# Windowed attention with a softplus layer: values in two 64-column tiles, w_out in four pieces, v loaded later

## The chip, the cores and the metric

The kernel runs on one core of one Trainium2 chip. The metric is the time of one execution in microseconds (us) of device time, as the median of several runs. A profiled execution gives a trace: every instruction of the five engines (PE is TensorE's matmul, PEld its weight load, DVE is VectorE, ACT ScalarE, POOL GpSimd, SP the queue that issues most DMAs), with the DMA packets and the clock that TensorE was granted. Times inside the trace are counted from the start of its span.

## What is computed

The reference in short: windowed attention with eight global positions over 8 batches, 8 heads, 576 positions and 64 elements a head, then a layer of width 2048 with softplus, from 4608 tokens of 512 back to 512.

```python
scores = q @ k.T / sqrt(64)                      # per batch and head
mask = |i - j| <= 32  or  i is global  or  j is global
attn = softmax(where(mask, scores, -1e9))
x = (attn @ v), heads side by side               # [4608, 512]
out = softplus(x @ w_in) @ w_out                 # w_in [512, 2048], w_out [2048, 512]
```

## The kernel before

A **unit** is 64 positions of one batch with all heads: 9 units a batch, 72 in all. A **group** (n4) is four units, and a **token tile** (m) is two groups, so 512 tokens, nine tiles in all. The head pairs are p = 0 to 3.

For each batch: k and q are loaded in bf16 by POOL's DMA queue (load_qk, L226; a cast rides in the DMA), v by SP's queue in float32 (load_v, L215), five pieces. POOL casts v into vA (add_cast, L446) and two DMAs on SP copy it, shifted by 64 positions, into vB (shift, L453 and L454). PE picks the rows of the global positions from k and q (pick, L473, 32-column tiles), and turns k and q (tk, L515; tq, L523, both in 64-column tiles); ACT or DVE copy the results into kx and qz.

For each unit: PE computes scores of 128 keys and 8 global keys (sc, L631, s), DVE adds the mask and takes the maximum (top, L637), ACT takes the exponential (ex, L658), DVE sums and inverts (su, L666 to L668), POOL normalises (no, L674, pn, and gc, L678), PE transposes (tp, L684) and ACT or DVE copy to pt. For each batch the global rows have a path of their own (add_global): scores sg (L557), mx on DVE (L564), exponentials gexp on ACT (L571), transposes tg (L585), values ov (L596), oz on DVE (L602).

For each group the **value stage** (val, L716 to L736) computes attention times v, turned, into xo. It accumulates, for each head pair, a product with the global values (L727, up to 256 columns wide) and one per unit with vA or vB (L734, 64 columns wide). In the kernel before each product is four matmuls of 128 rows and 32 output columns, one for each 32-column tile of the array:

```python
for c in range(4):
    r, h = slice(c * 32, (c + 1) * 32), slice(c // 2 * G, (c // 2 + 1) * G)
    nc.tensor.matmul(out=xo[r, y, x, :], lhsT=vw[:, p * P + c * 32:p * P + (c + 1) * 32],
                     rhs=PS["pt", n4 * 4 + x][:, p, h], start=False, stop=(x == e_ - 1))
```

xo is copied to xT (xev). For each token tile the layer follows (add_moe): first (h, L769), 16 chunks of 4 matmuls with w_in; softplus on ACT (L774); second (o, L779), for each of four 128-token rows 16 accumulating matmuls with w_out; then a copy (oev) and an output DMA from SP (L786).

The order of the work is not that of the loops. Every piece is a job with costs for the engines that can do it, dependences, a rank and buffers that it opens (`_Order.add`, L37), and `_Order.run` (L77) lays the jobs out greedily by its own estimate: at each step the job that can start first, and among these the one with the lowest rank, gets its engine. Each engine then works its list in that order and waits at the head of it. The estimate of a DMA job is its `moves` behind what its queue still has to move, plus `slack`. `SWITCH` (95 ns) is what the planner counts when PE changes from narrow tiles to the whole array and back, 1290 ns for a change of ACT's function table.

At the start of the kernel the queue of POOL carries k and q of batch 0, w_in in four pieces (L809), k and q of batch 1, then w_out in four pieces as one job (weights_out, L811), which waits for v of batch 1 in the plan; SP's queue carries v of batch 0, vB of batch 0, v of batch 1. A `hold` (L819) is a tiny DMA on SP that reads a tile just loaded, so that what is queued behind it on SP starts only when that tile has landed: v of batch 1 is held by q of batch 1.

Of the kernel before, what the change touches and what calls it, by code (L numbers as in the profile page):

```python
# [18 lines left out]
class _Order:  # L19
# [17 lines left out]
    def add(self, cost, emit, deps=(), rank=5, opens=(), uses=(), table=None, moves=0, tiled=False, slack=0):  # L37
# [39 lines left out]
    def run(self, free):  # L77
# [74 lines left out]
def kernel(  # L152
# [88 lines left out]
    nc.vector.tensor_copy(ident_b[:], ident[:])  # L241

# [182 lines left out]
    def add_load(b, which, deps):  # L425
        if which == 2:
            T["load", b, 2] = [o.add({"DMA": (100, 0)}, lambda e, x=x: load_v(b, x), deps, rank=0,
                                     opens=[("in_v", ("in", b, 2, x))], moves=1200, slack=3000 if b > 1 else 0) for x in range(NT5)]
            return
# [3 lines left out]
                                     lambda e: load_qk(b, which) if b else None, deps + early, rank=0, moves=4300, slack=4000 if b > 1 else 0)]  # L433

    def add_cast(b, engines):
# [19 lines left out]
        T["shift", b] = o.add({"DMA": (100, 0)}, shift, T["cast", b, 2] + early, rank=0, moves=1500, slack=2000 if b > 1 else 0)  # L455

    def add_prep(b, gate, rank):
# [38 lines left out]
        for n, ws in enumerate(steps):  # L496
            T["pick", b, n] = o.add({"PE": (460 * len(ws) + 190, 460 * len(ws) + 300)}, lambda e, ws=ws: pick(e, ws),
                                    [T["load", b, w][0] for w in ws] + [T.get(("pick", b, n - 1))], rank=4, tiled=True,
# [11 lines left out]
        for p in range(HP):  # L510
# [29 lines left out]
            T["tk", b, p] = o.add(mm(QR, NQ), tk, [T["load", b, 1][0], *gate], rank=rank, tiled=True, opens=[("tk", ("tk", b, p))])  # L540
            T["kev", b, p] = o.add({"ACT": (635, 720), "DVE": (800, 880)}, kev, [T["tk", b, p], *late, *blanks["g"]],
                                   rank=3, uses=[("tk", b, p)])
            T["tq", b, p] = o.add(mm(QR, NQ), tq, [T["load", b, 0][0], *gate], rank=rank, tiled=True, opens=[("tq", ("tq", b, p))])
# [5 lines left out]
    def add_global(b, gate, early):  # L549
# [55 lines left out]
        T["sg", b] = o.add({"PE": (390, 600)}, sg, ready + early, rank=3, tiled=True,  # L605
                           opens=[("sg", ("sg", b, 0)), ("sg", ("sg", b, 1)), ("small", ("m2", b))])
        both = [("sg", b, 0), ("sg", b, 1)]
        T["mx", b] = o.add({"DVE": (1114, 1300)}, mx, [T["sg", b]], rank=2, uses=both + [("m2", b)])
# [5 lines left out]
        T["ov", b] = o.add({"PE": (393, 600)}, ov, [T["lge", b], *T["cast", b, 2], T.get(("ones_g", b))], rank=3, tiled=True, opens=[("ov", ("ov", b))])  # L614
# [87 lines left out]
    def add_values(n4):  # L702
# [13 lines left out]
        def val(e):  # L716
            for half in range(2):
                xo = PS["xo", n4, half] = psum(("xo", n4, half), [P, 2, 4, G], FP32)
                for y in range(2):
                    p = half * 2 + y  # L720
                    u = 0
                    while u < 4:
                        b, j = divmod(n4 * 4 + u, NJ)
                        e_ = min(4, u + NJ - j)
                        for c in range(4):
                            r, h = slice(c * 32, (c + 1) * 32), slice(c // 2 * G, (c // 2 + 1) * G)
                            nc.tensor.matmul(out=xo[r, y, u:e_, :], lhsT=oz[b % 2][:, p, r],  # L727
                                             rhs=PS["R", n4][:, u:e_, h], start=True, stop=False)
                        for x in range(u, e_):
                            jx = j + x - u  # L730
                            vw = vA[b % 2][:, jx // 2, :] if jx % 2 == 0 else vB[b % 2][:, jx // 2, :]
                            for c in range(4):
                                r, h = slice(c * 32, (c + 1) * 32), slice(c // 2 * G, (c // 2 + 1) * G)
                                nc.tensor.matmul(out=xo[r, y, x, :], lhsT=vw[:, p * P + c * 32:p * P + (c + 1) * 32],  # L734
                                                 rhs=PS["pt", n4 * 4 + x][:, p, h], start=False, stop=(x == e_ - 1))
# [18 lines left out]
        T["val", n4] = o.add({"PE": (1030, 1190)}, val_, ready, rank=0, tiled=True,  # L754
# [7 lines left out]
    def add_moe(m, exps):  # L762
# [48 lines left out]
    def weights_out(e):  # L811
        for a in range(KF // 4):
            nc.gpsimd.dma_start(out=w_out_t[a][:, :, :],
                                in_=moe_w_out[a * 4 * P:(a + 1) * 4 * P, :].rearrange("(a p) m -> p a m", p=P))
# [13 lines left out]
    T["w_in"] = o.add({"POOL": (2150, 0)}, weights_in, [T["load", 0, 2][3]], rank=0, moves=10800)  # L828
# [14 lines left out]
    add_load(1, 2, [hold("w", [*T["load", 1, 0], T["shift", 0]], qn[1][0:1, 0, 0:16])])  # L843
    T["w_out"] = o.add({"POOL": (3000, 0)}, weights_out, [T["load", 1, 2][3]], rank=1, moves=12500)
# [18 lines left out]
    def make_batch(b, gate, rank):  # L863
# [12 lines left out]
    for m in range(len(TILES)):  # L876
# [8 lines left out]
        if m == 0:  # L885
            add_ones(1, [T["su", 5]])
# [9 lines left out]
        if nb < B:  # L896
            make_batch(nb, [T["ex", us[-1]]], 5)
# [31 lines left out]
```

## Time and profile before

| | us |
|---|---|
| median of three runs (402.34 to 409.56) | 404.95 |
| the profiled execution | 402.19 |
| its span, first to last instruction | 400.4 |
| PE busy (5152 matmuls) | 366.4 |
| ACT busy | 288.0 |
| DVE busy | 256.3 |
| POOL busy | 146.8 |

The page's strip cuts the span into 40 slices of about 10 us and gives each engine's busy share in tenths. A row of the timeline has the start, the time from the first start to the last end, engine, line, operation, the tiles as output <- input, the form, how many instructions are merged into it, and in brackets how long the engine had stood before it and what released it; "issue" means that the trace shows nothing it could have waited for. A row of the windows has the stretch and its length, then busy time and instruction count of PE, PEld, DVE, ACT and POOL, the granted clock, the share of the 16 DMA engines' time, and GB/s. A row of the groups ends with busy time, mean ns of one instruction, and the idle time before them. Matmuls overlap: what one adds to the time is the distance from its start to the next one's, not its own length.

### The profile page before, as it was taken

How to read it: one execution, taken by the hardware profiler on the slowest of the kernel's cores; microseconds unless marked ns; L12 is line 12 of the kernel's file. 1: busy time of each engine (PE TensorE's matmuls, PEld its weight loads, DVE VectorE, ACT ScalarE, POOL GpSimd, SP SyncE). 2: the span in 40 equal slices, each digit the busy share in tenths (PEclk: the TensorE clock that was granted, in tenths of full speed). 3: DMA queues.
4: the chain of work that ended last, by engine and by line, in shares of the span. 5: the costliest groups of instructions: out<-in, count | busy, mean ns of one | idle time of the engine just before them, and what ended most of it. 6: DMA issues, size and time to landing. Idle time of an engine off the chain costs nothing.

```text
span 400.4 us, 12909 instructions
## 1 busy us (share of the span) xinstructions
PE 366.4 (91%) x5152; PEld 204.6 (51%) x5152; DVE 256.3 (64%) x1093; ACT 288.0 (72%) x707; POOL 146.8 (37%) x265
## 2 busy tenths in 40 slices
PE   1866996996999999989999999999999999999996
PEld 1634752553555645555456545554466455545442
DVE  5798673854669837999488647984886478333011
ACT  2787668773589968967698769966997589595510
POOL 8986351680017700764146003830480036022000
PEclk9999999998999999999999999999999999999999
DMA  6899699959110394059758101079111011001012
GB/s 94 148 209 167 126 161 198 190 126 173 28 54 31 86 185 102 28 146 169 143 116 133 45 0 52 31 130 188 55 42 41 11 71 56 2 26 54 2 52 79
DMA packets 59467, 37.54 MB, mean 94 GB/s; under 512 B 42000, under 2 KB 53264, under 8 KB 59408
## 3 DMA queue, kind: packets, MB, share of 16 engines
q1 hardware_dynamic: 44176, 23.08, 23.3%
q0 software_dynamic: 15232, 13.65, 22.3%
q8 instruction: 40, 0.66, 0.7%
q14 instruction: 19, 0.16, 0.1%
HBM read 36.71 MB, written 9.44 MB: 115 GB/s over the span
## 4 chain that ended last, share of the span: by engine, by line
PE 61%; DVE 16%; DMA 7%; ACT 6%; issue 5%; POOL 4%; SPq 0%; DVEq 0%; POOLq 0%; ACTq 0%
PE h L769 31%; PE o L779 15%; DMA kn<-in_k_dram 6%; DVE sm L666 5%; PE s L631 3%; PE tp L684 3%; PE tk L515 2%; DVE rs L668 2%; ACT L571 2%; PE xo L727 2%; PE tq L523 2%; DVE st L637 2%; ACT pe L658 2%; PE xo L734 2%; POOL vA L446 2%
## 5 line engine op out<-in xcount | busy, mean ns | idle before, releaser
L674 POOL TENSOR_TENSOR pn<-pe,rs 128x512 bf16<-128x512 f32 x72 | 74.8, 1038 | 197.6 <-DVE rs L668 184.9
L779 PE MATMUL o<-wout,g 128*128 128x512 bf16 x576 | 142.0, 382 | 0.0
L769 PE MATMUL h<-xT,win 128*128 128x512 bf16 x576 | 138.3, 381 | 3.5 <-issue 3.5
L774 ACT ACTIVATE g<-h 128x512 bf16<-128x512 f32 x144 | 84.5, 597 | 54.8 <-PE h L769 46.7
L658 ACT ACTIVATE pe<-st,nb 128x136 f32<-128x136 f32 x288 | 92.9, 401 | 6.8 <-POOL gw L678 4.6
L637 DVE CUSTOM_DVE_ANT_0 st<-s,mask 128x136 f32<-128x136 f32 x288 | 70.1, 295 | 27.7 <-PE s L631 26.0
L769 PEld LDWEIGHTS <-win 128*128 128x128 bf16 x576 | 53.5, 98 | 55.4 <-issue 4.8
L779 PEld LDWEIGHTS <-g 128*128 128x128 bf16 x576 | 53.2, 98 | 50.2 <-issue 1.6
L666 DVE TENSOR_REDUCE sm<-pe 128x4 f32<-128x544 f32 x67 | 47.8, 713 | 12.0 <-ACT pe L658 11.7
L684 PE MATMUL tp<-ident_b,pn 128*128 128x128 bf16 x288 | 30.0, 231 | 9.6 <-POOL pn L674 6.8
L631 PE MATMUL s<-kx,qz 128*128 128x136 bf16 x288 | 35.5, 235 | 0.9 <-ACT qz L419 0.3
L631 PEld LDWEIGHTS <-qz 128*128 128x128 bf16 x288 | 24.4, 103 | 20.7 <-issue 4.1
L446 POOL CAST vA<-v 128x512 bf16<-128x512 f32 (+3 forms) x48 | 28.4, 611 | 16.9 <-DMA v<-in_v_dram 15.7
L684 PEld LDWEIGHTS <-pn 128*128 128x128 bf16 x288 | 19.6, 102 | 27.5 <-POOL pn L674 23.3
L419 DVE COPY osb<-o 128x512 f32<-128x512 f32 x18 | 12.4, 687 | 30.2 <-PE o L779 30.2
L419 DVE COPY qz<-tq 64x576 bf16<-64x576 bf16 x32 | 24.1, 753 | 4.8 <-PE tq L523 4.5
L637 DVE DVE_READ_ACCUMULATOR2_ANT nb<- 128x1 f32 x288 | 23.9, 83 | 0.0
L419 ACT COPY pt<-tp 128x512 bf16<-128x512 bf16 x34 | 19.4, 580 | 4.8 <-PE tp L684 4.7
L668 DVE TENSOR_SCALAR rs<-rs,notg 128x4 f32<-128x4 f32 x72 | 21.2, 294 | 2.6
L419 ACT COPY qz<-tq 64x576 bf16<-64x576 bf16 x32 | 20.4, 636 | 2.9 <-PE tq L523 2.6
L419 DVE COPY pt<-tp 128x512 bf16<-128x512 bf16 x38 | 15.9, 420 | 6.6 <-PE tp L684 6.2
L727 PE MATMUL xo<-R,oz 128*32 128x256 bf16 (+3 forms) x384 | 19.2, 259 | 0.3 <-DVE R L419 0.3
(120 smaller groups left out, 397.8 us busy)
## 6 DMA issues: line engine op xcount, KB each, us to landing
out_dram<-osb SPq DMA_DIRECT2D x36, 256.0 KB, 2.0
v<-in_v_dram SPq DMA_DIRECT2D x24, 256.0 KB, 7.1
kn<-in_k_dram POOLq DMA_DIRECT2D x8, 576.0 KB, 9.7
qn<-in_q_dram POOLq DMA_DIRECT2D x8, 576.0 KB, 12.9
vB<-vA SPq DMA_DIRECT2D x16, 256.0 KB, 3.8
v<-in_v_dram SPq DMA_DIRECT2D x16, 192.0 KB, 4.6
win<-in_moe_w_in_dram POOLq DMA_DIRECT2D x4, 512.0 KB, 9.6
wout<-in_moe_w_out_dram POOLq DMA_DIRECT2D x4, 512.0 KB, 12.2
```

The source lines that it names most:

```text
L419: (nc.scalar.copy if e == "ACT" else nc.vector.tensor_copy)(out, in_)
L446: nc.gpsimd.tensor_copy(to[r], at[r])
L631: nc.tensor.matmul(out=ps[:, y, :], lhsT=qz[i][:, x * 2 + y, j, :, :], rhs=kf[:, x * 2 + y, j * W:j * W + EXT], start=True, stop=True)
L637: nc.vector.tensor_tensor_reduce(out=PS["st", n][:, p, :], in0=PS["s", n, x][:, y, :], in1=mask[:, j, :], scale=-SCALE, scalar=3.0e38, op0 ...
L658: nc.scalar.activation(out=pe[:, p, 0:EXT], in_=PS["st", n][:, p, :], func=AF.Exp, bias=PS["nb", n][:, p:p + 1], scale=-1.0, **({"accum_ou ...
L666: nc.vector.reduce_sum(out=sm[:], in_=PS["pe", n][:, :, 0:EXT], axis=AX)
L668: nc.vector.tensor_scalar(out=rs[:], in0=rs[:], scalar1=notg[:, j:j + 1], scalar2=None, op0=OP.mult)
L674: nc.gpsimd.tensor_tensor(out=pn[:].rearrange("c p (a s) -> c p a s", a=2), in0=wide[:, :, :, 0:G], in1=rs[:].unsqueeze(2).unsqueeze(3).to ...
L684: nc.tensor.transpose(out=ps[:, p, :], in_=PS["pn", n][:, p, :], identity=ident_b[:])
L769: nc.tensor.matmul(out=h[:, :], lhsT=w_in_t[kd][:, c * P:(c + 1) * P], rhs=PS["xT", m][:, kd, :], start=(kd == 0), stop=(kd == KD - 1))
L774: nc.scalar.activation(out=t[:, :], in_=PS["h", m, c][:, :], func=AF.Softplus)
L779: nc.tensor.matmul(out=PS["o", m, ns][:, :], lhsT=PS["g", m, kf][:, ns * P:(ns + 1) * P], rhs=w_out_t[kf // 4][:, kf % 4, :], start=(kf == ...
```

## The change

The value stage uses two tiles of 64 columns in place of four of 32, so each product is two matmuls. The planner knows the two widths as 32 and 64 and counts SWITCH between them as well. w_out is four jobs, placed by units 4 to 7 of the plan, behind the second k and q in POOL's queue, and each second-layer matmul depends on its own piece; v of batch 1 is held by the second piece of w_out. The third k and q depend on the last piece of w_out. A small activation of its own (Exp on one column of zeros) stands at the head of ACT, and the planner starts with the exp table loaded. mx of batch 0 comes behind the scores of two units; the second ones job and the preparation of batch 1 change their dependence and rank; some loads get other slacks.

```diff
-        table = None
-        tiled = False
+        table = "exp"
+        tiled = 0
...
-                    t = max(t0, free[e] + (self.SWITCH if e == "PE" and tiled and not j["tiled"] else 0))
+                    t = max(t0, free[e] + (self.SWITCH if e == "PE" and tiled and tiled != j["tiled"] else 0))
...
-                if j["tiled"] and not tiled:
+                if not tiled and j["tiled"]:
...
+    warm = temp([P, 1], FP32, "warm")
+    nc.vector.memset(warm[:], 0.0)
+    nc.scalar.activation(out=warm[:], in_=warm[:], func=AF.Exp)
...
-                                     opens=[("in_v", ("in", b, 2, x))], moves=1200, slack=3000 if b > 1 else 0) for x in range(NT5)]
+                                     opens=[("in_v", ("in", b, 2, x))], moves=1200, slack=(0, 1500, 3000)[min(b, 2)]) for x in range(NT5)]
...
-        T["mx", b] = o.add({"DVE": (1114, 1300)}, mx, [T["sg", b]], rank=2, uses=both + [("m2", b)])
+        T["mx", b] = o.add({"DVE": (1114, 1300)}, mx, [T["sg", b], T["top", 1, 1] if b == 0 else None], rank=2, uses=both + [("m2", b)])
...
-                        for c in range(4):
-                            r, h = slice(c * 32, (c + 1) * 32), slice(c // 2 * G, (c // 2 + 1) * G)
+                        for h in range(2):
+                            r = slice(h * D, (h + 1) * D)
                             nc.tensor.matmul(out=xo[r, y, u:e_, :], lhsT=oz[b % 2][:, p, r],
-                                             rhs=PS["R", n4][:, u:e_, h], start=True, stop=False)
+                                             rhs=PS["R", n4][:, u:e_, h * G:(h + 1) * G], start=True, stop=False)
...
-                            for c in range(4):
-                                r, h = slice(c * 32, (c + 1) * 32), slice(c // 2 * G, (c // 2 + 1) * G)
-                                nc.tensor.matmul(out=xo[r, y, x, :], lhsT=vw[:, p * P + c * 32:p * P + (c + 1) * 32],
-                                                 rhs=PS["pt", n4 * 4 + x][:, p, h], start=False, stop=(x == e_ - 1))
+                            for h in range(2):
+                                r = slice(h * D, (h + 1) * D)
+                                nc.tensor.matmul(out=xo[r, y, x, :], lhsT=vw[:, p * P + h * D:p * P + (h + 1) * D],
+                                                 rhs=PS["pt", n4 * 4 + x][:, p, h * G:(h + 1) * G], start=False,
+                                                 stop=(x == e_ - 1))
...
-                             [T["soft", m, kf], T["w_out"], last, T["first", m, KF - 1] if m < len(TILES) - 1 else None],
+                             [T["soft", m, kf], T["w_out", kf // 4], last, T["first", m, KF - 1] if m < len(TILES) - 1 else None],
...
-    add_load(1, 2, [hold("w", [*T["load", 1, 0], T["shift", 0]], qn[1][0:1, 0, 0:16])])
-    T["w_out"] = o.add({"POOL": (3000, 0)}, weights_out, [T["load", 1, 2][3]], rank=1, moves=12500)
...
-                add_load(b, w, [T["no", (b - 2) * NJ + 2], T["shift", b - 1]])
+                add_load(b, w, [T["no", (b - 2) * NJ + 2], T["shift", b - 1] if b > 2 else T["w_out", KF // 4 - 1]])
...
-            add_ones(1, [T["su", 5]])
+            add_ones(1, [T["su", NJ - 1]])
+            for a in range(KF // 4):
+                T["w_out", a] = o.add({"POOL": (760, 0)}, lambda e, a=a: weights_out(a),
+                                      [T["no", 4 + a], T.get(("w_out", a - 1))], rank=1, moves=3100, slack=2000)
+            add_load(1, 2, [hold("w", [T["w_out", 1], T["shift", 0]], w_out_t[1][0:1, 0, 0:16])])
...
-            make_batch(nb, [T["ex", us[-1]]], 5)
+            make_batch(nb, [T["ex", us[-1]]], 4 if nb == 1 else 5)
```

As built, the order on PE changes mostly in the first token tiles. In the first, eight h stand ahead of the second pick, and 16 o of the tile's second layer stand directly behind its h, ahead of tg of batch 1; three and eight more o follow, then pick of batch 2 and ov. POOL issues the four w_out pieces between the units' normalisations (two behind unit 5, one behind unit 6, one behind unit 8), and the third k and q directly behind the last.

More of the change, by code (lines that the diff above doesn't have):

```diff
@@ L432, in add_load @@
         T["load", b, which] = [o.add({"POOL" if b else "DMA": (880 if b else 0, 0)},
-                                     lambda e: load_qk(b, which) if b else None, deps + early, rank=0, moves=4300, slack=4000 if b > 1 else 0)]
+                                     lambda e: load_qk(b, which) if b else None, deps + early, rank=0, moves=4300, slack=(0, 2500, 4000)[min(b, 2)])]
     def add_cast(b, engines):
@@ L454, in shift @@
             nc.sync.dma_start(out=vB[b % 2][64:P, :, :], in_=vA[b % 2][0:64, 1:NT5, :])
-        T["shift", b] = o.add({"DMA": (100, 0)}, shift, T["cast", b, 2] + early, rank=0, moves=1500, slack=2000 if b > 1 else 0)
+        T["shift", b] = o.add({"DMA": (100, 0)}, shift, T["cast", b, 2] + early, rank=0, moves=1500, slack=(0, 1000, 2000)[min(b, 2)])
     def add_prep(b, gate, rank):
@@ L826 @@
     add_load(0, 2, [hold("v", T["load", 0, 1], kn[0][0:1, 0, 0:16])])
-    T["w_in"] = o.add({"POOL": (2150, 0)}, weights_in, [T["load", 0, 2][3]], rank=0, moves=10800)
+    T["w_in"] = o.add({"POOL": (2150, 0)}, weights_in, [T["load", 0, 2][3]], rank=0, moves=10800, slack=1500)
     for w in (1, 0):
```

21 lines of the change are left out of this document (10 added, 11 removed).

## The prediction

> **What bounds the kernel.** I read the page's first two parts, then the timeline of TensorE (PE), then windows around each place where PE stood, and last the DMA issues on SP and POOL.
>
> ```profile
> span 400.4 us, 12909 instructions
> PE   1866996996999999989999999999999999999996
> q8 instruction: 40, 0.66, 0.7%
> ```
>
> From 40 us on nearly every tenth of the PE strip is a 9: behind the start, PE's own work sets the time. What can be gained is therefore where PE stands, where it runs at half clock, or work taken out of its queue. The strip dips in slice 6 and slice 9. The timeline of PE shows both, and two smaller ones of the second kind:
>
> ```profile
> 58.68 4.48 PE L769 MATMUL h<-xT,win 128*128 128x512 bf16 x20
> 65.80 0.71 PE L585 MATMUL tg<-ident_b,pg 128*128 128x128 bf16 x5 [2.65 <-ACT pg L571]
> 67.10 0.46 PE L596 MATMUL ov<-vA,lg 128*32 128x128 bf16 x20 [0.58 <-DVE lg L419]
> 67.74 3.59 PE L779 MATMUL o<-wout,g 128*128 128x512 bf16 x9
> 71.55 2.57 PE L779 MATMUL o<-wout,g 128*128 128x512 bf16 x11
> 77.75 0.21 PE L727 MATMUL xo<-R,oz 128*32 128x64 bf16 x4
> ...
> 91.79 0.81 PE L769 MATMUL h<-xT,win 128*128 128x512 bf16 x3
> 96.13 2.29 PE L769 MATMUL h<-xT,win 128*128 128x512 bf16 x5 [3.53 <-issue]
> ...
> 223.74 0.45 PE L523 MATMUL tq<-ident_b,qn 72*64 72x72 bf16 x16 [0.93 <-issue]
> ...
> 297.34 0.39 PE L515 MATMUL tk<-ident_b,kn 72*64 72x72 bf16 x12 [0.61 <-issue]
> ```
>
> Gap A, at 63 us: after the last h of the first token tile, PE waits 2.65 us for ACT's global exponentials and 0.58 us for DVE, then runs nine o in 3.59 us where the next eleven take 2.57. Gap B, at 92.6: 3.53 us in which nothing that the profile shows is waited for, then five h in 2.29 us where twenty took 4.48 before. The windows say why the matmuls behind both gaps are slow:
>
> ```profile
> 40.00:44.00 4.00, 4.00 (x152) 3.50 (x154) 2.63 (x14) 2.60 (x8) 0.00 (x0) 1.00 0.14 25
> 52.00:78.00 26.00, 22.68 (x180) 11.14 (x181) 15.75 (x75) 18.64 (x45) 9.26 (x15) 0.93 1.10 186
> 68.00:70.00 2.00, 2.00 (x7) 0.78 (x6) 1.81 (x7) 1.75 (x6) 1.16 (x2) 0.55 1.22 196
> 70.00:72.00 2.00, 2.00 (x10) 0.96 (x9) 1.34 (x4) 1.30 (x4) 0.61 (x2) 0.60 1.22 196
> 96.00:98.00 2.00, 1.87 (x5) 0.71 (x5) 0.00 (x0) 0.60 (x1) 0.00 (x0) 0.50 1.32 170
> ```
>
> The third number from the end is the granted clock: 0.55 and 0.60 behind gap A, 0.50 behind gap B. Both lie where the DMA share (next to last) is over 1.1. B I read as a late instruction fetch: the instruction queue fetches in 40 packets through the same loaded engines, and the gaps of 0.93 and 0.61 us "issue" also follow a value stage with 16-matmul transposes directly behind it, the places with most instructions per us. That reading is inferred; no row names it.
>
> **The change, part by part.**
>
> *Values in two column tiles.* The stage issues half as many matmuls. What a group of four 32-column matmuls takes, and what a pair of 64-column ones takes, stand in these rows of PE (the tk and tq transposes use 64-column tiles now):
>
> ```profile
> 85.14 0.28 PE L727 MATMUL xo<-R,oz 128*32 128x256 bf16 x4
> 85.25 0.20 PE L734 MATMUL xo<-pt,vB 128*32 128x64 bf16 x4
> ...
> 85.37 0.28 PE L727 MATMUL xo<-R,oz 128*32 128x256 bf16 x4
> ...
> 89.49 0.63 PE L473 MATMUL pick<-qn,pick 72*32 72x128 bf16 x32
> 89.95 0.62 PE L473 MATMUL pick<-kn,pick 72*32 72x128 bf16 x32
> 90.50 0.71 PE L523 MATMUL tq<-ident_b,qn 72*64 72x72 bf16 x32
> 91.04 0.69 PE L515 MATMUL tk<-ident_b,kn 72*64 72x72 bf16 x32
> ```
>
> Between 85.25 and 85.37 four groups start: 30 ns a group, 7 ns a matmul, so the four tiles run together. tq to tk: 0.54 us for 16 pairs, 34 ns a pair of 72 columns; scaled to 64 columns 30. The wide group (256 columns, 85.14 to 85.25) takes 0.11 us, 0.43 ns a column, 27.5 ns for 64. So a pair is bounded by 27.5 and 34 against 30 now. How many groups there are:
>
> ```profile
> L727 PE MATMUL xo<-R,oz 128*32 128x256 bf16 (+3 forms) x384 | 19.2, 259 | 0.3 <-DVE R L419 0.3
> ...
> L734 PE MATMUL xo<-pt,vA 128*32 128x64 bf16 x640 | 18.5, 199 | 0.0
> L734 PE MATMUL xo<-pt,vB 128*32 128x64 bf16 x512 | 17.6, 199 | 0.0
> ...
> L515 PEld LDWEIGHTS <-kn 72*64 72x64 bf16 x512 | 12.2, 124 | 3.9 <-issue 1.8 <-DMA kn<-in_k_dram 1.4
> L734 PEld LDWEIGHTS <-vA 128*32 128x32 bf16 x640 | 14.5, 101 | 0.1
> ```
>
> (640+512)/4 = 288 narrow groups: 288 x (27.5 to 34, less 30) = -0.7 to +1.2 us for the whole kernel. I take 0: halving the matmuls by itself buys nothing, because they already overlap. What it does buy is a mode switch: 32-column pick to 64-column tq costs 0.55 where pick to pick costs 0.46, so 0.09 us; in the order as built ten value stages now stand directly beside a tk or tq, 10 x 0.09 = -0.9 us. And PE's instruction stream loses 768 matmuls with their weight loads, all in the densest stretches: I take the gaps of 0.93 and 0.61 away, -1.5 us (ends 0 and -1.5).
>
> [...]
>
> *w_out in four pieces behind the second q, v of that batch beside it.* These rows carry it:
>
> ```profile
> 20.60 17.64 DMA kn<-in_k_dram
> ...
> 42.00 0.54 SPq L821 DMA_DIRECT2D held<-qn  x1
> 42.58 4.46 SPq L219 DMA_DIRECT2D v<-in_v_dram  x5
> ...
> 49.23 3.09 POOL L813 DMA_DIRECT2D wout<-in_moe_w_out_dram  x4
> ...
> DMA to landing us min/median/max: 6.1/12.2/16.6
> ...
> 54.22 0.86 POOL L227 DMA_DIRECT2D qn<-in_q_dram  x1
> ...
> DMA to landing us min/median/max: 24.0/24.0/24.0
> ...
> 54.17 20.67 SPq L219 DMA_DIRECT2D v<-in_v_dram  x5
> ...
> DMA to landing us min/median/max: 7.7/8.4/9.1
> ...
> 79.35 3.08 POOL L446 CAST vA<-v 32x512 bf16<-32x512 f32 x5
> ```
>
> (First landing row: w_out's four; second: the third q; third: the two vB copies of batch 1.) Batch 1's q lands at 42.0; then the DMA engines are nearly idle (share 0.14 in 40 to 44) until v, and POOL's queue moves nothing before 49.2. w_out lands from 55.3 to 68.1, (68.1-55.3)/3 = 4.3 us a piece. Behind the q its pieces would land at about 46, 50, 55 and 59, and the third k and q, queued behind them, at about 64 and 69. So 16 o can stand ahead of tg, and in the order as built they do, then 3 and 8 more before ov, with pick between. Gap A goes: 2.65 + 0.58, and the half clock behind it, 3.59 less 9 x 2.57/11 = 2.10, so 1.5: together -4.7 us. The filler isn't lost to later stages: from 67 to 92 PE never stood, so every o done early shortens that stretch, as long as ACT, DVE and POOL bring the units.
>
> What is late next is v of batch 1. It is issued when the second w_out piece has landed, near 50 instead of 42.6, and must be cast by POOL before ov, copied into vB before the third value stage, and in POOL's queue its casts stand ahead of the first pn of the stage. Alone v is quick; beside POOL's queue it starves: the third v, issued from 54.17, was cast only at 79.35, when the q of 54.22 had landed (78.2). If bytes are conserved: 17 + 10 us of w_out, k and q with half of v beside them, the rest of v done by about 69. PE reaches ov near 70. That is tight; pick, which needs the third q at 69, as well. I take +1.5 us, ends 0 and the price of the rival below. SP: the first out goes ahead of vB's copies, ready near 67, so they wait for the cast, not for it.
>
> POOL now issues four pieces of 0.77 us between the units 5 and 9: 3.1 us later for the last pn of the second value stage. Cover: in the order that stage stands behind tk of batch 1, which waits for k to land at 38.2 either way; I take 0, without that cover 3.1. The eight h that now go ahead of the second pick are work moved, not removed: 0. With these queues drained by 69, loads and fetches of the 92 us stretch start against a shorter backlog, and the dense stretch before it has half its value matmuls and pick no longer in it: I take gap B as gone, 3.53 and 2.29 less 5 x 4.48/20 = 1.2, -4.7 us; ends 0 and -4.7.
>
> *Exp table, mx, ranks, slacks.* ACT already loads one table at its start and none before the first exponential, so the warm use removes nothing: one memset and one activation under the first k load, 0. mx behind two units' scores gives ACT an earlier start under the same k load, 0. The switch and slack numbers only move the order; from the fifth tile's second layer on it is the same as before but for the value stages.
>
> Sum: -0.9 - 1.5 - 4.7 - 4.7 + 1.5 = -10.3 us. The profiled execution took 402.19 us (span 400.4), so 391.9. The median of the runs is 404.95, 2.8 above it; shifted with it the sum is 394.6. I predict between, 393.
>
> **The rivals.**
> 1. *Gap B stays or moves.* Against it the thinner stream; for it, k, q and v of batch 3 still go out together near 85, and the order still has value, tk, tq directly there. Then 393 + 4.7 = 398. Chance 0.17.
> 2. *A new wait takes A's place*, at pick or ov, with about the same length and the same half clock: 393 + 4.7 = 398. For it, the 69 against 70. Chance 0.10.
> 3. *v starves: slower.* If v of batch 1 needs as long beside w_out, k and q as the third v (25 us from issue to cast), it is cast at 75 to 78 and vB lands 8.4 later, at 83.5 to 86.5; the third value stage, at 77.75 now, comes 6 to 9 us late, and nothing is left to fill. With B's fetch in the same congestion nothing else is won: 405 + 6 to 9 = 411 to 414. It decides from v's last cast after 69 (then vB's 8.4 us end at 77.75). Against it: v's own bytes are small and POOL's queue is done near 69. Chance 0.11.
> 4. *Pairs bound by weight loads.* The row of 64-column loads has 124 ns against 101: 23 ns more, unhidden in 384 groups (288 and 384/4) = 8.8: 402. Chance 0.05; the tq row speaks against it. [...]
> 5. *Every matmul has its price.* At tq's 17 ns a matmul, 768 fewer give 13: 380. Chance 0.03; 7 ns a matmul speaks against it. [...]
>
> **How the numbers follow.** The forecast has 0.54; its own range is 387 (no new wait, loads a little earlier) to 397 (one of the small terms 0, 1.5 more of wait). The range takes in 1, 2 and 4: 386 to 404. Outside lie 3 and 5 and a little of the forecast, under 0.2. A measurement of this kernel tells about 2% from no change, 396.9 to 413. Faster: 0.54 less 0.02, rival 5, and a few hundredths of 1 and 2: 0.58. Slower: half of rival 3 and a rest, 0.07. Within: 0.35.
>
> **What would show it.** Value stage: groups of two near 30 ns apart, its length unchanged but for the switch. A: no idle time before tg after the first tile, clock 1.0 in 60 to 72, o at 61 to 65. w_out landed by 60. v of batch 1 cast by 69 and ov without wait; a wait there on POOL vA or at pick on the q is rival 2 or 3. B: no "issue" of over 1 us on PE between 80 and 100. Wrong would be the prediction if PE stands as long as before in other places, above all between 66 and 78.

## The result and the profile after

The kernel after takes 389.71 us (median of four runs, 389.29 to 389.95), the kernel before 407.25 beside it on the same chip (four runs, 402.34 to 410.08). The ratio is 0.9654, 95% interval [0.9598, 0.9709]: 3.5% faster. Ratios here and below leave out runs that lie over 1.5% above the fastest of their kernel, so beside the widely scattered runs of the kernel before a ratio and the quotient of two medians need not agree.

What PE waited for without a visible cause stands first in the waits (engine, line and what it waited for: total us, how often, the longest). Of the kernel before:

```profile
PE h L769 <- issue: 3.5, 1, 3.5
...
PE tq L523 <- issue: 1.3, 2, 0.9
...
PE tk L515 <- issue: 0.6, 1, 0.6
```

And all that is left of it in the kernel after, and three lines of its page:

```profile
PE xo L739 <- issue: 0.3, 1, 0.3
```

```profile
span 387.8 us, 11381 instructions
...
PE   1945999999998999999999999999999999999996
...
q8 instruction: 34, 0.56, 0.6%
```

5.4 us of "issue" have become 0.3, the dip of slice 9 is gone, and the instruction queue fetches 34 packets in place of 40. The other dip, behind the first token tile, is gone as well; the timeline of PE and two windows of the kernel after:

```profile
61.54 1.89 PE L775 MATMUL h<-xT,win 128*128 128x512 bf16 x8
63.26 3.62 PE L785 MATMUL o<-wout,g 128*128 128x512 bf16 x16
66.72 0.44 PE L590 MATMUL tg<-ident_b,pg 128*128 128x128 bf16 x5
...
70.72 0.47 PE L601 MATMUL ov<-vA,lg 128*32 128x128 bf16 x20
...
72.20 0.40 PE L689 MATMUL tp<-ident_b,pn 128*128 128x128 bf16 x4 [0.25 <-POOL pn L679]
```

```profile
60.00:72.00 12.00, 11.96 (x149) 6.44 (x146) 7.03 (x35) 10.31 (x30) 4.07 (x7) 1.00 0.26 62
...
80.00:100.00 20.00, 19.50 (x279) 11.40 (x277) 15.24 (x70) 16.40 (x35) 9.54 (x16) 1.00 0.67 126
```

Sixteen o fill the place where PE stood 2.65 us for tg, and the granted clock is 1.00 in both windows.

### The profile page after: what moved, and what is told of

Same layout as the page of the kernel before. It is cut to its first block, busy times and chain, and to the rows that moved or that the text cites. A ratio compares the mean times of both kernels' runs of the same rounds, so it can differ in the third digit from the quotient of the medians.

```text
span 387.8 us, 11381 instructions
## 1 busy us (share of the span) xinstructions
PE 360.8 (93%) x4384; PEld 203.8 (53%) x4384; DVE 256.1 (66%) x1086; ACT 289.1 (75%) x716; POOL 147.2 (38%) x265
## 4 chain that ended last, share of the span: by engine, by line
PE 51%; DVE 18%; ACT 10%; DMA 7%; POOL 5%; issue 4%; SPq 4%; DVEq 0%; POOLq 0%; ACTq 0%
PE h L775 25%; PE o L785 12%; DVE sm L671 5%; ACT pe L663 5%; DMA v<-in_v_dram 5%; SPq L219 4%; DVE rs L673 3%; PE s L636 3%; DVE st L642 3%; PE tp L689 2%; DMA qn<-in_q_dram 2%; POOL pn L679 2%; POOL vA L451 2%; PE xo L732 2%; PE xo L739 2%
## 5 line engine op out<-in xcount | busy, mean ns | idle before, releaser
L785 PE MATMUL o<-wout,g 128*128 128x512 bf16 x576 | 140.1, 379 | 0.0
L671 DVE TENSOR_REDUCE sm<-pe 128x4 f32<-128x544 f32 x67 | 47.8, 713 | 12.4 <-ACT pe L663 12.1
L636 PE MATMUL s<-kx,qz 128*128 128x136 bf16 x288 | 34.0, 234 | 0.4 <-POOL vA L451 0.3
L424 DVE COPY qz<-tq 64x576 bf16<-64x576 bf16 x36 | 27.1, 753 | 3.0 <-PE tq L528 2.5
L424 ACT COPY pt<-tp 128x512 bf16<-128x512 bf16 x37 | 21.4, 586 | 4.9 <-PE tp L689 4.8
L673 DVE TENSOR_SCALAR rs<-rs,notg 128x4 f32<-128x4 f32 x72 | 21.7, 301 | 2.7 <-DVE rs L672 0.2
L732 PE MATMUL xo<-R,oz 128*64 128x256 bf16 (+3 forms) x192 | 19.8, 263 | 1.2 <-ACT R L424 0.7
L582 DVE TENSOR_TENSOR s<-s 128x1 f32<-128x1 f32 x8 | 1.3, 158 | 28.1 <-ACT pg L576 28.1
L739 PE MATMUL xo<-pt,vA 128*64 128x64 bf16 x320 | 19.1, 201 | 0.0
## 6 DMA issues: line engine op xcount, KB each, us to landing
wout<-in_moe_w_out_dram POOLq DMA_DIRECT2D x4, 512.0 KB, 11.6
```

The costliest lines, as they stand in the source:

```text
L424: (nc.scalar.copy if e == "ACT" else nc.vector.tensor_copy)(out, in_)
L636: nc.tensor.matmul(out=ps[:, y, :], lhsT=qz[i][:, x * 2 + y, j, :, :], rhs=kf[:, x * 2 + y, j * W:j * W + EXT], start=True, stop=True)
L671: nc.vector.reduce_sum(out=sm[:], in_=PS["pe", n][:, :, 0:EXT], axis=AX)
L673: nc.vector.tensor_scalar(out=rs[:], in0=rs[:], scalar1=notg[:, j:j + 1], scalar2=None, op0=OP.mult)
L785: nc.tensor.matmul(out=PS["o", m, ns][:, :], lhsT=PS["g", m, kf][:, ns * P:(ns + 1) * P], rhs=w_out_t[kf // 4][:, kf % 4, :], start=(kf == ...
```

## The experiments

All medians, with the range of the runs. The kernel before ran beside them on the same chip: it took 405.23 (402.11 to 414.26) beside the first four, 403.50 (396.21 to 409.54) beside the next four, 404.13 (398.34 to 405.45) beside the last four.

| run | us | range | ratio to before |
|---|---|---|---|
| e1_after_four_tiles | 399.64 | 395.54 to 401.15 | 0.9870 [0.9803, 0.9937] |
| e2_before_two_tiles | 394.81 | 394.64 to 396.46 | 0.9765 [0.9722, 0.9809] |
| e3_after_w_out_late | 393.72 | 393.62 to 394.10 | 0.9742 [0.9705, 0.9778] |
| e6_before_w_out_early | 400.97 | 397.75 to 404.74 | 0.9919 [0.9871, 0.9966] |
| e8_four_tiles_beside_tk | 399.27 | 397.45 to 402.57 | 0.9992 [0.9937, 1.0047] |
| e9_four_tiles_elsewhere | 389.29 | 388.31 to 390.35 | 0.9696 [0.9631, 0.9762] |
| after_again | 389.27 | 388.61 to 389.69 | 0.9694 [0.9633, 0.9755] |
| e4_kq_before_w_in | 389.13 | 388.62 to 389.68 | 0.9689 [0.9611, 0.9766] |
| e10_e8_without_late_loads | 393.68 | 392.95 to 394.26 | 0.9799 [0.9727, 0.9870] |
| e11_after_without_late_loads | 389.39 | 389.00 to 389.50 | 0.9689 [0.9604, 0.9775] |
| e7_v_held_by_q | 389.15 | 388.91 to 389.47 | 0.9688 [0.9635, 0.9741] |
| e5_no_exp_warm | 394.73 | 390.88 to 395.49 | 0.9800 [0.9724, 0.9876] |

### The two halves of the change, each alone

**The value tiles put back, the rest of the change kept** (e1_after_four_tiles; the planner still counts 64-column tiles, so the order on every engine is that of the kernel after):

```diff
-                        for h in range(2):
-                            r = slice(h * D, (h + 1) * D)
+                        for c in range(4):
+                            r, h = slice(c * 32, (c + 1) * 32), slice(c // 2 * G, (c // 2 + 1) * G)
...
```

> The changed kernel with its order unchanged, but each product of the value stage again four 32-column matmuls (the planner still told 64, so that no other instruction moves). Theory 'stream': the gaps called issue went because PE has 768 fewer matmuls to fetch; then one to four gaps of 0.3 to 3.5 us come back, 392 to 396 us in all, some with the label issue on PE between 84 and 100 us. Theory 'load': they went because w_out, k, q and v are queued otherwise; then no such gap over 0.5 us and only the switches come back, 9 x 0.09 = 0.8, less 18 x 0.045 that the pairs are slower inside (936 ns a stage against 894): 389.7 us, no change. In either case the stage by itself is shown to be worth nothing if its inner length falls back to 894 ns and its exit to 123 ns.

**The value tiles alone, on the kernel before** (e2_before_two_tiles; the same edit the other way round in the value stage of the kernel before, its order kept):

> The kernel before with its order unchanged, but each product of the value stage two 64-column matmuls. Theory 'stream': gap B (3.5 us and 1.4 of half clock) and the gaps of 0.9 and 0.6 us go, span near 394 us. Theory 'load': gap B stays, span 399.5 to 401 us, and only the two small gaps may go. Gap A (2.65 us before tg, 0.58 before ov, half clock behind) stays in both.

**w_out early alone, on the kernel before** (e6_before_w_out_early; four tiles; for the changed jobs the planner lays out another order):

```diff
...
-    add_load(1, 2, [hold("w", [*T["load", 1, 0], T["shift", 0]], qn[1][0:1, 0, 0:16])])
-    T["w_out"] = o.add({"POOL": (3000, 0)}, weights_out, [T["load", 1, 2][3]], rank=1, moves=12500)
...
+            for a in range(KF // 4):
+                T["w_out", a] = o.add({"POOL": (760, 0)}, lambda e, a=a: weights_out(a),
+                                      [T["no", 4 + a], T.get(("w_out", a - 1))], rank=1, moves=3100, slack=2000)
+            add_load(1, 2, [hold("w", [T["w_out", 1], T["shift", 0]], w_out_t[1][0:1, 0, 0:16])])
```

> The kernel before with only w_out in four pieces behind the second q and v held by its second piece; value stage, table and slacks as before. My theory: gap A goes, and since the loads around 85 to 100 us move as well, part of gap B: span 391 to 396 us. Rival 'values': most of the 12.6 us come from the value stage and its instruction stream, so 396 to 399 us with gap B still there.

The four corners: 405.23 before, 400.97 with w_out early (-4.3; 1.4 to 5.2 by the interval of the ratio), 394.81 with two tiles (-10.4), 389.7 with both and the small parts (-15.5, where the two alone add up to -14.7). The tiles are the greater part, in either order: 399.64 less 389.71 is 9.9. The median of e1 lies above the 392 to 396 that its theory 'stream' expected (its profiled execution, 395.54, within). The span of e6, 398.2, misses the 391 to 396 of its first theory and lies in the 396 to 399 of the rival 'values'.

That the two add up does not mean that each is worth this by itself. e5 (below) has both halves and the small parts and only lacks the planner's flag for the exp table with its activation; it takes 394.73, no less than e2. It has no gap A either, but its first h starts at 49.03, where that of e2 starts near 46.3. So beside two tiles w_out early paid only with the order that the flag is argued to bring.

Of these kernels those with four tiles spread over 5.6 to 12 us, those with two over less than 2. Below, e5 spreads over 4.6 with two tiles, and e10, with four tiles in half of the stages but without the later loads, over 1.3. The waits of PE say where the time was; first e1 (four tiles), then e6 (four tiles), then e2 (two tiles):

```profile
PE h L774 <- issue: 3.1, 4, 2.1
...
PE tk L520 <- issue: 1.6, 2, 1.3
...
PE o L784 <- issue: 0.5, 3, 0.2
```

```profile
PE tq L523 <- issue: 2.2, 1, 2.2
PE tk L515 <- issue: 2.0, 2, 1.4
...
PE o L779 <- issue: 1.1, 4, 0.6
...
PE h L769 <- issue: 0.8, 2, 0.5
```

```profile
PE o L780 <- issue: 1.0, 6, 0.2
```

With four tiles there are stops of up to 2.2 us, the long ones in tk, tq or the h soon behind them. In e2 none is over 0.2 us, and its six of that size are no stops: its trace holds 4334 matmuls and 4384 weight loads, so records of matmuls are missing. (The longest in another two-tile kernel is 0.6 us, in e4 below.) Gap B is gone in e2 though its w_out is as late as before. In e6, whose w_out is early, the stop at the place of gap B is down to 0.26 us, but others come: its stops of over 0.25 us make 5.6 us in all, those of the kernel before 5.4. So what gap B cost hung on the tiles; with w_out early and four tiles the stops only lie elsewhere. Gap A hung on w_out. The rows of e6, of e2 and of e5:

```profile
69.96 3.62 PE L779 MATMUL o<-wout,g 128*128 128x512 bf16 x16
73.41 0.44 PE L585 MATMUL tg<-ident_b,pg 128*128 128x128 bf16 x5
```

```profile
65.98 0.82 PE L585 MATMUL tg<-ident_b,pg 128*128 128x128 bf16 x5 [2.65 <-ACT pg L571]
```

```profile
67.66 3.62 PE L782 MATMUL o<-wout,g 128*128 128x512 bf16 x16
71.11 0.44 PE L587 MATMUL tg<-ident_b,pg 128*128 128x128 bf16 x5
```

**w_out back behind v, the rest of the change kept** (e3_after_w_out_late):

```diff
+    add_load(1, 2, [hold("w", [*T["load", 1, 0], T["shift", 0]], qn[1][0:1, 0, 0:16])])
+    for a in range(KF // 4):
+        T["w_out", a] = o.add({"POOL": (760, 0)}, lambda e, a=a: weights_out(a),
+                              [T["load", 1, 2][3] if a == 0 else T["w_out", a - 1]], rank=1, moves=3100, slack=2000)
...
-            for a in range(KF // 4):
-                T["w_out", a] = o.add({"POOL": (760, 0)}, lambda e, a=a: weights_out(a),
-                                      [T["no", 4 + a], T.get(("w_out", a - 1))], rank=1, moves=3100, slack=2000)
-            add_load(1, 2, [hold("w", [T["w_out", 1], T["shift", 0]], w_out_t[1][0:1, 0, 0:16])])
```

> The changed kernel, but w_out's four pieces are again behind v of batch 1, and v is held by q as before. My theory: w_out then lands 8 to 10 us later, 55 to 68 us, nine and not sixteen o stand ahead of tg, and 3 to 5 us of the gain go: 393 to 396 us. Rival: the gain comes from the order (table, switch, slacks) and not from where w_out is: 389 to 391 us.

It costs 4.0 us against the kernel after. The timeline of PE shows nine o where sixteen stood, and three waits:

```profile
63.18 2.11 PE L785 MATMUL o<-wout,g 128*128 128x512 bf16 x9
65.99 0.71 PE L590 MATMUL tg<-ident_b,pg 128*128 128x128 bf16 x5 [0.70 <-ACT pg L576]
...
70.12 0.40 PE L689 MATMUL tp<-ident_b,pn 128*128 128x128 bf16 x4 [0.31 <-POOL pn L679]
...
72.75 0.40 PE L689 MATMUL tp<-ident_b,pn 128*128 128x128 bf16 x4 [0.94 <-POOL pn L679]
```

These make 1.95 us against 0.25 in the kernel after; the rest of the 4.0 is spread over many waits behind 80 us, none of them over 1.2. The planner answers the later w_out with another order, so the 4.0 us are the price of both.

### Why four tiles stop PE: by position

The instruction queue's packets are 16 KB (0.66 MB in the 40 of the kernel before). The kernel before gives PE 10304 matmuls and weight loads and has 40 packets, the kernel after 8768 and 34: 1536 fewer instructions in 6 packets fewer, so 256 in a packet. If a packet is late, four tiles must hurt where PE uses up a packet fast, so where a value stage and the 64 small transposes of tk and tq follow each other, and not where the same stage stands between h and o. Two kernels put the four tiles back in nine of the eighteen value stages each, with after's order:

```diff
+            FOUR = (1, 3, 5, 8, 9, 10, 11, 12, 14)     # e8; e9 has (0, 2, 4, 6, 7, 13, 15, 16, 17)
...
-                        for h in range(2):
-                            r = slice(h * D, (h + 1) * D)
+                        w = 32 if n4 in FOUR else D
+                        for c in range(P // w):
+                            r, h = slice(c * w, (c + 1) * w), c * w // D
...
```

> The kernel after, with the four 32-column tiles back in nine of the eighteen value stages: those that have tk or tq as a direct neighbour (368 matmuls more than after; order and loads as after). Theory 'stream' (PE stands because the next packet of its instructions is late, where a value stage and the 64 small transposes of tk and tq use up a packet in under 2 us): all of the loss of about 10 us that four tiles everywhere cost in this order (399.6 against 389.7) comes back here, so 396 to 402, the runs several us apart, and waits of 'issue' of 1 us and more on PE within a few us behind these stages. Theory 'per matmul' (each 32-column matmul costs its own time wherever it stands): half of the loss, 394 to 395, with no 'issue' waits. Theory 'nothing' (the four-tile kernel lost its time for another reason): 389.7.

> The kernel after, with four 32-column tiles back in the other nine value stages, those that stand between o, tp, h and s and not beside tk or tq (400 matmuls more than after, so a few more than the run before has). Theory 'stream': these stages have long matmuls on both sides, so a packet lasts several us; about after's time, 389 to 391, runs within 1 us, 'issue' on PE under 1 us in all. Theory 'per matmul': a little over half of the loss, 394 to 396.

> The kernel after, unchanged, beside the other kernels of this call on the same chip. All theories: 389 to 391 and runs within 1 us, if the difference between chips is small.

e8, with 368 matmuls more, loses all of it: 399.27 against 389.27 of the kernel after on the same chip. e9, with 400 more, loses nothing: 389.29. The range of e8 and that of e9 are 7 us apart. A price for each matmul is excluded. (The nine stages of e8 also pay the change from 32 to 64 columns, 0.09 us each, which those of e9 don't: 0.8 of the 10.) One stop of e8, on its timeline of PE, and the clock behind it:

```profile
209.93 0.43 PE L520 MATMUL tk<-ident_b,kn 72*64 72x72 bf16 x16
210.19 0.29 PE L528 MATMUL tq<-ident_b,qn 72*64 72x72 bf16 x7
214.88 0.51 PE L528 MATMUL tq<-ident_b,qn 72*64 72x72 bf16 x9 [4.40 <-issue]
```

```profile
215.00:220.00 5.00, 4.78 (x31) 3.01 (x33) 2.67 (x7) 0.60 (x1) 0.00 (x0) 0.50 0.08 17
```

PE stops after the seventh of sixteen equal transposes, with nothing to wait for, and runs at half clock behind the stop while the DMA engines are nearly idle (share 0.08). So here the half clock follows a long stop without loaded engines. In the DMA view of e8, the stretch from 207.9 to 212.6 has no packet of the instruction queue, and the next 1.1 us have one:

```profile
DMA packets 160, 0.20 MB, mean 181 GB/s; under 512 B 7, under 2 KB 133, under 8 KB 159
...
q8 instruction: 1, 0.02, 5.4%
```

The packet starts at 212.69, when PE has stood for over 2 us, and is there at 213.64; PE goes on at 214.88, 1.24 us later. In the kernel before it is the same at gap B: packet from 93.56 to 94.67, PE again at 96.13.

All the stops show it. In the fourteen profiled executions PE has 24 waits on "issue" of over 0.25 us. Counted in blocks of 128 weight loads, which with as many matmuls are 256 instructions, each of the 24 begins at 0.67 to 0.73 of a block, so at one place of the block whatever PE is doing there, and each ends 1.2 to 1.6 us after a packet of the instruction queue has landed. No packet starts earlier than some 1.2 blocks before PE needs it.

From this the course of a packet can be estimated. When it is asked for is not in the trace; as an estimate from these starts the ask is put at 0.625 of a block, some 1.1 blocks before PE needs the packet. 57 of 489 packets start earlier than that, so the ask is rather too late, and the second and third column are rough, to about 1 us. The places that matter (us; "used up" is the life of the packet that PE then works on, "landed" is from the ask to the end of the transfer):

| kernel, place | used up in | landed after (estimate) | PE stood |
|---|---|---|---|
| before, 88.3 | 3.1 | 6.4 | 3.53 |
| e1, 210.3 | 3.7 | 4.0 | 1.25 |
| e8, 207.8 | 2.3 | 5.8 | 4.40 |
| e10 (below), 206.4 | 2.3 | 2.7 | 1.48 |
| after, 205.0 | 5.4 | 4.6 | 0.33 |

By this estimate PE stands where landing, and the 1.2 to 1.6 us after it, take longer than the packet lasts. With four tiles a packet lasts 1.9 to 3.7 us in the dense places, with two tiles 3.5 us or more. At 262.5 us of the kernel before (3.1 against 4.1) and at 85.1 of e1 (2.3 against 2.5) the estimate asks for a stop, and the waits there, 0.25 and 0.35 us, are put down to DVE and ACT; they too end 1.3 us after the landing.

The price of e8 can be added up as well. Its span is 11.5 us longer than that of after_again (398.4 against 386.9). PE stands 5.0 us more behind 40 us (12.1 against 7.1), and the granted clock is half until 50.05 us where after_again has it full from 44.25, and again from 214.88 to 220.71. PE works in some 10.8 of these 11.6 us, and an h takes about twice as long at half clock (four in 1.92 us against 1.03, below), so they cost some 5.4. With 0.8 for the changes of width the estimate is 11.2 of the 11.5.

### Is it the loaded DMA engines?

**e8 and the kernel after without the k, q and v of the third and fourth batch** (e10, e11; these batches are computed from what the first two left):

```diff
-lambda e, x=x: load_v(b, x), deps, rank=0,
+lambda e, x=x: load_v(b, x) if b < 2 else None, deps, rank=0,
...
-lambda e: load_qk(b, which) if b else None
+lambda e: load_qk(b, which) if b == 1 else None
...
-to, at = vA[b % 2][:, n, :], PS["in", b, 2, n][:, :]
+to, at = vA[b % 2][:, n, :], PS["in", min(b, 1), 2, n][:, :]
```

> The kernel of e8_four_tiles_beside_tk (399.3 us) without the loads of k, q and v of the third and fourth batch; those batches are computed from what the first two left in the same tiles, so the results of these batches are not the reference's. The instructions of PE, ACT and DVE and their order are the same as in e8. Theory 'late packet behind loaded DMA engines' (a packet of 256 PE instructions starts within about 1 us when the DMA engines are idle and 3 to 5 us late when they are busy; in the dense stages a packet lasts 2.2 us): with the loads gone the stalls of 'issue' of 1 us and more behind 90 us go, and the kernel comes to 386 to 391, no further from the next run of this call than 2 us. Theory 'dense stretch alone' (PE stands there whatever the DMA engines do): the waits of 'issue' stay, 396 to 400.

> The control of the run before: the kernel after without the loads of k, q and v of the third and fourth batch (results of these batches are not the reference's; PE, ACT and DVE have the same instructions in the same order as after). All theories: PE hardly waited for these loads in after, so 386 to 390. What it gains against after is what the loads cost otherwise; the difference between it and the run before is what is left of the four tiles.

Both expectations for e10 miss: 393.68 lies between 386 to 391 and 396 to 400. The windows around the estimated ask, e8 and then e10, and the stop of e10:

```profile
207.80:212.70 4.90, 2.68 (x138) 2.04 (x136) 3.35 (x11) 4.87 (x13) 2.47 (x4) 1.00 1.08 186
```

```profile
206.40:208.90 2.50, 2.50 (x138) 2.00 (x136) 2.20 (x6) 2.50 (x9) 0.70 (x1) 1.00 0.03 7
```

```profile
208.75 0.30 PE L528 MATMUL tq<-ident_b,qn 72*64 72x72 bf16 x7
210.53 0.35 PE L528 MATMUL tq<-ident_b,qn 72*64 72x72 bf16 x9 [1.48 <-issue]
```

The same instructions stop at the same transpose, for 4.40 us at a DMA share of 1.08 and for 1.48 us at 0.03. So two things make the stop: the stretch is short enough that even a packet on idle engines is late, by 1.48 us, and loaded engines add 2.9. Over the profiled executions, with the ask estimated as above, a packet landed 1.7 us after it (median of 158; middle half 0.8 to 2.0) where the share from ask to landing was under 0.05, and 4.3 us (median of 152; 3.0 to 5.5) where it was over 0.9. In the kernel after, where the packet at 205.0 lasts 5.4 us, the loads cost nothing: without them it takes 389.39. The 4.0 us between the spans of e10 and e11 (391.8 and 387.8) are 2.4 more of "issue", the 1.48 and one of 0.9 at 44 us, where loads still run (DMA share 1.20 from 38 to 50 us), and a half clock behind the latter that lasts longer: granted clock 0.57 against 0.72 from 38 to 50 us, 12 x 0.15 = 1.8.

### The small parts and a further idea

**v of batch 1 held by its q, as before** (e7_v_held_by_q) and **no warm use, the planner told of no table** (e5_no_exp_warm):

```diff
-            add_load(1, 2, [hold("w", [T["w_out", 1], T["shift", 0]], w_out_t[1][0:1, 0, 0:16])])
+            add_load(1, 2, [hold("w", [*T["load", 1, 0], T["shift", 0]], qn[1][0:1, 0, 0:16])])
```

> The kernel after, with v of batch 1 held back by its q again, as in the kernel before, instead of by the second piece of w_out; w_out's pieces stay early. Theory 'v in time anyway' (in after v was cast by 62.7, 8 us before ov): no gain from v earlier, and w_out's pieces share the engines with v, about 1 to 2 us later each: 389 to 391. Rival 'v takes the bytes of w_out': the o ahead of tg find their piece late, and part of the idle time before tg comes back: 391 to 393.

```diff
-        table = "exp"
+        table = None
...
-    warm = temp([P, 1], FP32, "warm")
-    nc.vector.memset(warm[:], 0.0)
-    nc.scalar.activation(out=warm[:], in_=warm[:], func=AF.Exp)
```

> The kernel after without the use that loads the exp table and with the planner told of no table at the start, as in the kernel before. As predicted, the table part is worth nothing: 389 to 390. Rival: the first exponential waits for its table under a wait that PE feels, 391.

e7 is the same as the kernel after: the place of v is worth nothing. (Its expectation puts v's cast at 62.7; that holds for four of the five pieces only, the last is cast from 70.30 in the kernel after.) e5 misses both ways: 394.73, 5 us slower. ACT loads its first table at the same moment with the warm use (first row, kernel after) and without (second row), and no other before the first layer's softplus:

```profile
0.81 1.28 ACT L246 ACT_TABLE_LOAD   x1 [0.81 <-PEq L920]
```

```profile
0.82 1.28 ACT L421 ACT_TABLE_LOAD   x1 [0.82 <-PEq L917]
```

So the activation moves no table load. But the planner, told of a load of 1290 ns that does not come, lays the start out in another way: pick and tq of batch 1 go ahead of the first h, which starts at 49.03 and not at 44.33, and PE works at half speed for longer: four h of e5 take 1.92 us at 50.93, and 1.03 from 55.51 on:

```profile
50.93 1.92 PE L772 MATMUL h<-xT,win 128*128 128x512 bf16 x4
```

The h of the second tile starts 5.3 us later (92.1 against 86.8 in after_again), so most of the 6.6 us between the two spans (393.5 and 386.9) is there by then. That the order is the cause is argued from this trace; the two edits were not run apart. Why two of the six runs of e5 took 391 and four 395 stays open.

**k and q of batch 1 ahead of w_in in POOL's queue** (e4_kq_before_w_in), an attempt at a faster kernel:

```diff
-    T["w_in"] = o.add({"POOL": (2150, 0)}, weights_in, [T["load", 0, 2][3]], rank=0, moves=10800, slack=1500)
     for w in (1, 0):
-        add_load(1, w, [T["w_in"]])
+        add_load(1, w, [T["load", 0, 2][3]])
+    T["w_in"] = o.add({"POOL": (2150, 0)}, weights_in, [T["load", 1, 0][0]], rank=0, moves=10800, slack=1500)
```

> The kernel after, with k and q of batch 1 queued ahead of w_in instead of behind it; pick, tk and tq of batch 1 then stand ahead of the second value stage, and the first h behind it. Theory 'bytes' (until 44 us the DMA engines set the time and the order of the bytes only decides what PE has to do meanwhile): the 8.6 us in which PE waits for the k of batch 1 shrink to 2 to 5, the first h comes at 45 to 48 instead of 44.3 but less of the small work stands behind it: 386 to 389. Theory 'PE has no filler' (until w_in is there nothing but small work can run, and this is done either way): the first h comes later by the time of k and q, 4 us, with nothing back: 391 to 394.

389.13, no difference, and just outside both ranges, 386 to 389 and 391 to 394. The first h starts 1.7 us later, at 46.02, with less behind it. The 8.5 us wait that the expectation names is that of the first batch's k, which this edit does not touch; the expectation read the row wrongly. No version here beats the kernel after.

## Why the prediction was right, step by step

The forecast, 393 in 386 to 404 and faster, holds at 389.71. By its steps:

- **Value stage at 0, switch -0.9.** Half right. The groups are 31 ns apart, as these rows of the kernel after show, the tk behind them 30 ns after the last:

```profile
83.92 0.20 PE L739 MATMUL xo<-pt,vA 128*64 128x64 bf16 x2
83.95 0.20 PE L739 MATMUL xo<-pt,vB 128*64 128x64 bf16 x2
...
84.69 0.20 PE L739 MATMUL xo<-pt,vA 128*64 128x64 bf16 x2
84.72 0.43 PE L520 MATMUL tk<-ident_b,kn 72*64 72x72 bf16 x16
```

  A stage of 40 takes 936 ns from first to last start in place of 894 for 80, about +0.7 us over sixteen stages; the exit to tk or tq takes 28 ns in place of 123. So the switch came, beside nine stages and not ten, but the stages took about as much back: with their edges, and the waits in them, the sixteen take 21.7 us against 21.6. The halved matmuls by themselves bought nothing, and e9 shows it by time.
- **Rivals 4 and 5.** Both fell. The loads of 64 columns take longer than those of 32 (101), and lie hidden:

```profile
L739 PEld LDWEIGHTS <-vA 128*64 128x64 bf16 x320 | 15.9, 116 | 0.0
```

  A pair every 31 ns is less than the 116 ns of one load, so the loads run beside each other. The 400 more matmuls of e9 cost nothing (389.29 against 389.27), so here a matmul has no price of its own.
- **The two "issue" gaps -1.5 and gap B -4.7.** Right, and the runs fit the late fetch that the prediction inferred: each of the 24 stops ends 1.2 to 1.6 us after an instruction packet has landed, and e2 has none of these gaps. Its median of 394.81 against the 402.19 that the sum started from gives -7.4, for -7.1 of these steps with the switch; its profiled execution, 396.46, gives -5.7. Of the two reasons given for B, the thinner stream is enough by itself (e2); drained queues with four tiles leave as much "issue" as before (e6). The half clock behind the gaps, put beside a DMA share of over 1.1, does not need it: in e8 the clock is 0.50 behind the stop of 4.40 us at a share of 0.08.
- **Gap A -4.7.** The wait went, and through w_out, as said. The price is right for the order as built, +4.0 by e3, and not for w_out alone: the -4.3 of e6 come with a first h at 50.81, and e5 has no gap A and gains nothing on e2.
- **The new wait, +1.5.** Mis-sized: 0.25. The step took 4.3 us for a piece of w_out from the row in which v shared the engines; here the four pieces land at 44.1, 46.6, 49.1 and 51.8, about 2.5 us each. The third k and q, issued at 41.05 and 41.89, land at 58.1 and 59.2, not at 64 and 69:

```profile
41.05 0.86 POOL L227 DMA_DIRECT2D kn<-in_k_dram  x1
41.89 0.83 POOL L227 DMA_DIRECT2D qn<-in_q_dram  x1
...
70.30 0.60 POOL L451 CAST vA<-v 96x512 bf16<-96x512 f32 x1
```

  v was as tight as said: the last piece is cast from 70.30, though it had landed by 62.2, and ov starts at 70.72. It did not wait.
- **The exp table at 0.** Right for the activation, but its flag in the planner carries, as argued above, an order that is worth 5 us (e5). The prediction costed the order as built, so its sum took that order for granted and did not see what the flag was worth.
- **393 from 391.9 and 394.6.** Here the forecast lost what the sum had. It shifted half way to the median of the runs, 2.8 above the profiled execution. That excess was probably the thing the change removes, late packets, more of them in some runs than in others; with one profile for each kernel this is argued from the spreads, not shown. The sum of -10.3 should have grown with the median: e2 alone is -7.4 against the profiled execution and -10.4 against the median. From one profiled execution to the other it is -12.7, 2.4 more than the sum: 1.2 of it is the wait that did not come, 0.4 a third stop of the kernel before, in tq at 45 us, that the list leaves out, and the rest stays open.

## What to carry to other kernels

Where PE stands on "issue" in the middle of equal small matmuls, count its instructions: here 256 of them, matmuls and weight loads, used up in 2 to 4 us were not replaced in time, and fewer instructions there were the cure. Fewer, wider column tiles did that at no cost in time, and position decided: some 400 more matmuls cost nothing between long ones and 10 us beside other short ones. A kernel whose runs scatter by per cents (here 402.34 to 410.08 before, 389.29 to 389.95 after) may owe the scatter to the very stall that a change removes, so a gain may be larger against the median than against the one profiled execution.

## What the runs showed of the hardware that was not expected

- The transfer of a 16 KB packet of the instruction queue takes 0.9 to 1.8 us (kernels before and after), and at the 24 stops PE goes on 1.2 to 1.6 us after it.
- Two long stops on "issue" cost more than their wait: the granted clock was half for 3.4 us around the end of the 3.53 of the kernel before (95.50 to 98.91) and for 6.8 us around that of the 4.40 of e8 (213.88 to 220.71). Behind the 1.48 of e10 and the 2.13 of e1 it stayed at 1.00.
- In e10 the DMA engines moved nothing from 206.5 to 207.9, and the packet started only at 207.94, about 1.5 us after its ask as estimated above.
- Two 64-column products start every 31 ns, four 32-column ones every 29 (kernels after and before); from a value stage to tk, which has 64-column tiles, it takes 28 ns from 64 columns and 123 from 32, so the change costs 95 ns.
